# Half blocks put behind a condition, and wider matmuls in the experts' second product

## The chip, the cores and the metric

The kernel runs on one core of a Trainium2 chip. The metric is the device time of one execution in microseconds. Three runs of the kernel before took 5778.13, 5779.1 and 5784.61 us (median 5779.1). The engines are PE (TensorE, the matmuls), ACT (ScalarE), DVE (VectorE), POOL (GpSimd, which issues the gathers and scatters) and SP (SyncE, which issues the other transfers).

## The reference, cut to what matters

```python
attn = np.maximum((1/S) * z @ z.T, 0) ** 2       # 8 batches, S = 3072
x = (u * (attn @ v)).reshape(24576, 256)
h = x @ w_in; x = (h - np.tanh(h)) @ w_out       # 256 -> 2048 -> 256
e_idx = np.argmax(x @ w_gate, axis=1)            # one of 8 experts for each token
for e in range(8):
    mask = e_idx == e
    h = np.maximum(x[mask] @ w1[e], 0)           # 256 -> 1024
    out[mask] = gate_w[mask, None] * eom[mask, e, None] * (h @ w2[e])   # 1024 -> 256
```

The change touches only the last part, the experts.

## The kernel before, in words

**Stages.** Attention, the dense layer and the routing run chunk by chunk (48 chunks of 512 tokens) until about 4.45 ms. The routing writes each token's number into a table, sorted by expert. Then the experts run over blocks of that table: `NA` = 39 whole blocks of 512 tokens (i = 0 to 38), then `NHB` = 25 half blocks of 256 (i = 39 to 63). How many half blocks hold tokens depends on the data: 24576 - 39*512 = 4608 tokens are left, 18 half blocks if every expert's rest fills its blocks, and up to 7 more, since each of 8 experts may leave its last one part empty. `end[E-1]` is that count. The kernel before runs all 25; a half block without tokens reads and computes zeros, and its scatter drops the rows.

**Precision.** Each float32 operand is split into a high and a low part. A product is three matmuls: high by high, high by low, low by high.

**One block.** `b_load` fetches token numbers (SP), `x_load` gathers the tokens' rows (POOL, one DMA for each 128 tokens), `w_fetch` loads both weights (SP; a half block loads the second one whole and `w_split` splits it on ACT, DVE and POOL), `x_tr` transposes on PE and evacuates on ACT and DVE. Then come four groups g: `w1_mm` (12 matmuls; 512 columns wide in a whole block, 256 in a half one), `h_make` (the relu on ACT, the low part on DVE), `w2_mm` (for each of 2 features and each slice t of 128 tokens 3 matmuls of 256 columns: 24 in a whole block, 12 in a half one). `y_out` scales the result (ACT, one instruction for each slice) into `yo`, a tile with one buffer, and scatters it (POOL).

**What sets the order.** Every step is entered with a due time (`at(t, ...)`), and all steps are recorded in the order of these; the numbers are a plan, not measured. Every engine then runs its own instructions in that order. `w2_mm` of group g is due two groups behind `w1_mm` of g, so that between the last `w2_mm` of block i and the first of block i+1 stands one `w1_mm` group of block i+1.

**PSUM.** The result of `w2_mm` takes two banks in a whole block (two slices in each): `av0`, `av1` in the first five blocks, from then on these and `x20`, `x21` in turn; in a half block one bank, `x20` and `x21` in turn. `x_tr` and every second `w1_mm` share a buffer with the tag `sc`, so a `w1_mm` waits there until DVE has read the transposes (L795).

Of the kernel before, what the change touches and what calls it, by code (L numbers as in the profile page):

```python
# [5 lines left out]
F32 = mybir.dt.float32  # L6
F32R = mybir.dt.float32r
BF16 = mybir.dt.bfloat16
I32 = mybir.dt.int32
I64 = mybir.dt.int64  # L10
U16 = mybir.dt.uint16
AF = mybir.ActivationFunctionType
ALU = mybir.AluOpType
# [4 lines left out]
P = 128  # L18
FLOOR = 2.0**-15
CH = 512  # L20
# [5 lines left out]
    HA=(1, 7), L0=((), (0, 2, 4, 6, 8, 10)), LP=(0, 2, 4, 6, 8, 9, 10),  # L26
    G2=3.0, G3=5.0, GT=130.0, C0=6.0, C1=14.0, WL=14.0, CA=11.0, CP=15.0, ES=70.0,
    B0=30.0, B1=31.0, BL=14.0, XL=26.0, L1=2.0, L2=2.0, IO=10.0, SP=5.0, F0=24.0, F1=12.0,
    Z0=3.0, V0=40.0, V1=11.0, X1=1.0, RX=18.0,
)  # L30


# [28 lines left out]
def build(tc, u, v, z, w_in, w_out, w_gate, w_ogate, w1, w2, out):  # L61
    nc = tc.nc
    B, S, D = u.shape
    DQ = z.shape[2]
    N = B * S
    F = w_in.shape[1]
    E = w_gate.shape[1]
# [6 lines left out]
    NF2 = F2 // P  # L74
    CAP = N + CH
    HB = CH // 2
    NA = max(0, NCH - 2 - (E - 1))
    NHB = (N - NA * CH) // HB + E - 1
    assert ND == 2 and DQ == 64 and E == 8
    pb, pk, pc = _fit()  # L80

# [4 lines left out]
    tasks = []  # L86

    def at(t, fn, *a):
        tasks.append((t, len(tasks), fn, a))

    def flush():
        tasks.sort(key=lambda x: (x[0], x[1]))
        for _, _, fn, a in tasks:
            fn(*a)
        tasks.clear()
# [3 lines left out]
    def free_order(key, inst):  # L99

        i = inst.ins
        tc.declare_no_dep(i, group=key, reason="rows of different tokens")
        tc.add_to_no_dep_group(key, i)

    top = ExitStack()
    const = top.enter_context(tc.tile_pool(name="const", bufs=1))
# [40 lines left out]
    with ExitStack() as st:  # L147
# [3 lines left out]
        ps_s, ps_h, ps_a, ps_x = pp("ps_s", 1), pp("ps_h", 1), pp("ps_a", 1), pp("ps_x", 1)  # L151
# [411 lines left out]
        K = SCHED  # L563
# [11 lines left out]
        for b in range(B):  # L575
            for g in range(NG):
                if b == 0:
                    tz = -60.0 + g * K["Z0"]
                    tzt, tv = tz + 2, tz + K["V0"] + g * K["V1"]
                else:  # L580
                    t0 = (b * NG - 1) * TC
# [7 lines left out]
        for fp in range(NFP):  # L589
            t = K["C0"] + K["C1"] * fp  # L590
# [7 lines left out]
        for n, c in enumerate([c for c in range(3, NCH - 3) if c % NG != NG - 1][: 4 * E]):  # L598
            t = c * TC + K["ES"]
            at(t - 20.0, e_load, n // 4, n // 2 % 2, n % 2)  # L600
            at(t, e_split, n // 4, n // 2 % 2, n % 2)
        for c in range(NCH):
            t0 = c * TC
# [3 lines left out]
            for p in range(NJP):  # L607
                t = t0 + p * DJ
# [6 lines left out]
            for f in range(NFP):  # L615
                t = tm0 + f * DF
# [10 lines left out]
            n = int((te + 4.0 - EX - t0) // DJ) + 1  # L627
# [24 lines left out]
        less = [const.tile([1, E], F32, name=f"less{k}") for k in range(2)]  # L652
        it = const.tile([1, TBN], F32, name="it")
        iti = const.tile([1, TBN], I32, name="iti")
        tbe = [const.tile([1, TBN], I32, name=f"tbe{k}") for k in range(2)]
        tbb = [const.tile([1, TBN], I32, name=f"tbb{k}") for k in range(2)]

# [40 lines left out]
        def table_out(half):  # L698
            nb, end, sta, ex_, bs = (tb[n] for n in ("nb", "end", "sta", "ex", "bs"))
            tt, ts_ = nc.vector.tensor_tensor, nc.vector.tensor_scalar  # L700

            ts_(bs, bs, float(E * CAP), None, op0=ALU.min)
            nc.vector.tensor_copy(tbb[half], bs)
            ts_(ex_, ex_, float(E - 1), None, op0=ALU.min)
            nc.vector.tensor_copy(tbe[half], ex_)
            if not half:
                tt(sta, end, nb, op=ALU.subtract)
                ts_(sta, sta, float(NA), None, op0=ALU.min)
                ts_(end, end, float(NA), None, op0=ALU.min)
                tt(used[:, 0:E], end, sta, op=ALU.subtract)  # L710

        def block_table(t, half):

            at(t, table_counts, half)
            at(t + 2.0, table_steps, half)
            for e in range(E):
                at(t + 4.0 + e, table_expert, half, e)
            at(t + 13.0, table_out, half)
            return t + 13.0

        IDS, XG, WR, WB, XT, HS, YP = {}, {}, {}, {}, {}, {}, {}
        cp = {}

        def nt(i):
            return 4 if i < NA else 2
# [104 lines left out]

        def w2_mm(i, g):
            b2, hh = WB[i, 1], HS.pop((i, g))
            if g == 0:

                q = [int(k % 2 and k > 3) for k in range(NA)] + [NA % 2] * NHB
                pool, tags = ((ps_a, ("av0", "av1")), (ps_x, ("x20", "x21")))[q[i]]
                tags = tags if i < NA else tags[i % 2 : i % 2 + 1]
                YP[i] = [pool.tile([P, 2, D], F32, tag=x, name=f"y{x}") for x in tags]
            for j in range(2):
                f = 2 * g + j  # L840
                for t in range(nt(i)):
                    dst = YP[i][t // 2][:, t % 2]
                    for n, (a, w) in enumerate(((0, 0), (0, 1), (1, 0))):
                        nc.tensor.matmul(  # L844
                            dst, hh[:, a, j, t * P : (t + 1) * P], b2[:, w, f],
                            start=(f == 0 and n == 0 and t % 2 == 0),
                            stop=(f == NF2 - 1 and n == 2), skip_group_check=True,
                        )

        def y_out(i):  # L850
            ids, sc = IDS.pop(i)
            yo = cp[1].tile([P, 4, D], F32, tag="yo", name="yo")
            for t in range(nt(i)):
                nc.scalar.activation(  # L854
                    yo[:, t], YP[i][t // 2][:, t % 2], AF.Copy, scale=sc[:, t : t + 1]
                )
            for t in range(nt(i)):
                free_order("out", nc.gpsimd.indirect_dma_start(  # L858
                    out, bass.IndirectOffsetOnAxis(ap=ids[:, t : t + 1], axis=0),
                    yo[:, t], None, bounds_check=N - 1, oob_is_err=False,  # L860
                ))
            del YP[i], WB[i, 0], WB[i, 1], XT[i]
# [5 lines left out]
        t_table = T_ROUTED[NCH - 3] if NA else T_ROUTED[NCH - 1] - 13.0  # L868
        block_table(t_table + 0.1, 0)
        t_table = block_table(T_ROUTED[NCH - 1] + 0.2, 1)  # L870
        tC = NCH * TC + LA + 3.0
        t0 = tC + K["B0"]
        for i in range(NA + NHB):
            TB = 22.0 if i < NA else 11.0
            if i == NA:
                t0 = max(t0, t_table + 50.0)
            tf = t0 - (28 if i < NA else 20)
            at(max(t0 - K["F0"] if i < NA else t0 - K["F1"], tC), w_fetch, i, 0)
            at(max(t0 - 14.0 if i < NA else tf, tC), w_fetch, i, 1)
            at(max(tf - K["BL"], tC - 20.0), b_load, i)  # L880
            at(max(t0 - (K["XL"] if i < NA else 15.0), tC), x_load, i)
            first = i < min(NA, 3)
            for part in range(2 if i >= NA else 0):
                at(t0 - K["SP"] + 2.5 * part, w_split, i, part)
            if i == 0:
                at(t0 - 5.0 - K["X1"], x_tr, i)
            L2 = K["L1"] if i < NA else K["L2"]
            NG2 = NF2 // 2
            DB = TB / NG2
            for g in range(NG2):  # L890
                at(t0 + g * DB, w1_mm, i, g)
                at(t0 + g * DB + 0.4 * DB, h_make, i, g)
                at(t0 + (g + L2) * DB, w2_mm, i, g)
            at(t0 + (NG2 + L2 - 0.5) * DB, y_out, i)
            if i + 1 < NA + NHB:
                at(t0 + 2.7 * DB, x_tr, i + 1)
            t0 += K["B1"] if i < min(NA, 2) else TB

        late = [x for x in tasks if x[0] >= tC - 0.2]
        tasks[:] = [x for x in tasks if x[0] < tC - 0.2]  # L900
        with tc.manual_schedule():
# [4 lines left out]
        tasks.extend(late)  # L906
        with tc.manual_schedule():
            flush()
    top.close()


# [23 lines left out]
```

## Time and profile before

| what | value |
|---|---|
| three runs | 5778.13, 5779.1, 5784.61 us |
| the profiled execution | 5780.38 us, of it a span of 5778.7 us |
| PE busy | 5686.3 us (98%) |
| DVE, ACT, POOL busy | 4144.9, 3560.0, 1803.6 us (72%, 62%, 31%) |
| DMA | 872 MB, 151 GB/s in the mean |

PE is busy 98% of the span, and the other engines less in the experts' stage than ahead of it. A busy PE still holds matmuls of different cost, so the experts' stage is read by the starts of its matmul groups. In rows of the timeline the columns are the start in us, the duration in us, engine, line and operation, tiles and shape, count, and in brackets the idle time ahead of it with what ended it.

### The profile page before, as it was taken

To read this page: it belongs to the slowest core of one execution; us is meant where nothing else is said; L and a number is where in the kernel's file an instruction comes from. 1 tells how busy PE (TensorE), PEld (TensorE's weight loads), DVE (VectorE), ACT (ScalarE), POOL (GpSimd) and SP (SyncE) were. 2 spreads that over 40 slices of the span, in tenths; PEclk is the share of its full clock that TensorE was granted. 3 is DMA by queue.
4 is the path that set the end of the run, shared out by engine and by line. 5 is a ranking of instruction groups with operands and counts; after the bars stand their busy time and mean duration, and the time that the engine had idled before them with its cause. 6 is when DMAs were issued, how large, how long until landed. Compare 5 with 4: busy or idle time off the path is not lost. (4 is left out here: it accounts for less than half of the span.)

```text
span 5778.7 us, 73965 instructions
## 1 busy us (share of the span) xinstructions
PE 5686.3 (98%) x28444; PEld 4752.4 (82%) x28444; DVE 4144.9 (72%) x4921; ACT 3560.0 (62%) x3941; POOL 1803.6 (31%) x1174
## 2 busy tenths in 40 slices
PE   7999999999999999999999999999999999999999
PEld 5887888788888888888888788878887789999999
DVE  7888888888888888888888888888888532222233
ACT  5767776777677767777777767776766322222344
POOL 2224222322332224233322322242222233333355
PEclk9999999999999999999999999999999999999999
DMA  5333333333433333333333333343333566666687
GB/s 203 102 127 134 121 128 130 130 129 119 137 127 122 122 139 128 115 132 134 126 120 128 135 126 125 123 137 112 99 112 116 206 219 224 228 230 224 231 288 246
DMA packets 194065, 872.24 MB, mean 151 GB/s; under 512 B 37354, under 2 KB 78448, under 8 KB 130352
## 3 DMA queue, kind: packets, MB, share of 16 engines
q1 hardware_dynamic: 157936, 769.87, 38.2%
q0 software_dynamic: 35776, 97.63, 5.5%
q8 instruction: 225, 3.69, 0.3%
q14 instruction: 128, 1.05, 0.1%
HBM read 757.16 MB, written 99.49 MB: 148 GB/s over the span
## 5 line engine op out<-in xcount | busy, mean ns | idle before, releaser
L355 POOL TENSOR_TENSOR a<-r,a 128x1024 fp32r<-128x1024 f32 x328 | 789.5, 2407 | 2644.3 <-DVE a L352 2637.4
L400 PE MATMUL h<-x,ws 128*128 128x512 f32 x4608 | 1188.9, 397 | 18.5 <-DVE x L380 7.4
L341 ACT ACTIVATE r<-sc 128x1024 f32<-128x1024 f32 x576 | 586.6, 1018 | 976.8 <-PE sc L336 973.6
L400 PEld LDWEIGHTS h<-x,ws 128*128 128x128 f32 x4608 | 862.3, 188 | 225.3 <-DVE x L380 10.9
L371 PE MATMUL av<-a,v 128*128 128x512 f32 x2304 | 906.2, 393 | 11.4 <-DVE a L355 8.0
L370 PE MATMUL av<-a,v 128*128 128x512 f32 x2304 | 906.6, 394 | 2.2 <-ACT a L350 1.2
L372 PE MATMUL av<-a,v 128*128 128x512 f32 x2304 | 902.3, 392 | 0.0
L825 DVE SCALAR_TENSOR_TENSOR hh<-h,hh 128x1024 fp32r<-128x1024 f32 (+1 forms) x256 | 260.2, 1016 | 819.8 <-ACT hh L824 819.8
L824 ACT ACTIVATE hh<-h 128x1024 fp32r<-128x1024 f32 (+1 forms) x256 | 220.2, 860 | 820.1 <-PE h L813 820.1
L813 PE MATMUL h<-xt,b 128*128 128x512 f32 (+1 forms) x3072 | 622.1, 352 | 9.5 <-DVE xt L795 8.5
L342 ACT ACTIVATE r<-r 128x1024 f32<-128x1024 f32 x576 | 611.9, 1062 | 18.3
L439 PE MATMUL x<-g,ws 128*128 128x512 f32 x1536 | 611.7, 398 | 5.3 <-DVE g L426 3.0
L440 PE MATMUL x<-g,ws 128*128 128x512 f32 x1536 | 610.6, 398 | 6.1 <-DVE g L427 5.7
L408 DVE TENSOR_TENSOR gd<-h,gd 128x1024 f32<-128x1024 f32 x384 | 468.9, 1221 | 202.1 <-ACT gs L407 202.1
L441 PE MATMUL x<-g,ws 128*128 128x512 f32 x1536 | 607.8, 396 | 0.0
L813 PEld LDWEIGHTS h<-xt,b 128*128 128x128 f32 x3072 | 493.4, 190 | 81.9 <-DVE xt L795 13.6
L352 DVE CAST a<-r 128x1024 fp32r<-128x1024 f32 x470 | 335.6, 714 | 307.0 <-ACT r L342 186.0
L423 DVE SCALAR_TENSOR_TENSOR gq<-gt,gq 128x1024 f32<-128x1024 f32 x384 | 516.4, 1345 | 53.3 <-ACT gt L418 29.4
L424 DVE COPY_PREDICATED gq<-gm,gd 128x1024 f32<-128x1024 uint16 x384 | 518.4, 1350 | 13.2
L371 PEld LDWEIGHTS av<-a,v 128*128 128x128 f32 x2304 | 435.7, 189 | 108.2 <-DVE a L355 11.3
L370 PEld LDWEIGHTS av<-a,v 128*128 128x128 f32 x2304 | 435.1, 189 | 101.0 <-ACT a L350 3.6
L372 PEld LDWEIGHTS av<-a,v 128*128 128x128 f32 x2304 | 435.3, 189 | 93.9
(145 smaller groups left out, 9499.4 us busy)
## 6 DMA issues: line engine op xcount, KB each, us to landing
ws<-wsd SPq DMA_DIRECT2D x384, 1024.0 KB, 4.9
b<-wsp SPq DMA_DIRECT2D x103, 2048.0 KB, 8.2
wsp<-el POOLq DMA_DIRECT2D x32, 1024.0 KB, 8.5
x2d<-rows SPq DMA_DIRECT2D x48, 576.0 KB, 4.8
wr<-in_moe_w SPq DMA_DIRECT2D x25, 1024.0 KB, 9.6
vr<-in_v SPq DMA_DIRECT2D x48, 512.0 KB, 5.8
ur<-in_u SPq DMA_DIRECT2D x48, 512.0 KB, 5.8
er<-in_moe_w SPq DMA_DIRECT2D x32, 512.0 KB, 6.0
```

What stands on the lines that cost most here:

```text
L341: nc.scalar.activation(r, RR.pop((c, p)), AF.Relu, scale=1.0 / S)
L342: nc.scalar.activation(r, r, AF.Square)
L355: eng.tensor_tensor(a[:, 1], r, a[:, 0].bitcast(F32), op=ALU.subtract)
L370: nc.tensor.matmul(dst, vh, a[:, 0, k], start=(J == 0), stop=False)
L371: nc.tensor.matmul(dst, vh, a[:, 1, k], start=False, stop=False)
L372: nc.tensor.matmul(dst, vl, a[:, 0, k], start=False, stop=(J == 2 * NJP - 1))
L400: nc.tensor.matmul(ps, w, xx, start=(n == 0), stop=(n == 5))
L424: nc.vector.copy_predicated(q, m.bitcast(U16), d)
L439: nc.tensor.matmul(dst, wh, gg[:, 0, i], start=first, stop=False)
L440: nc.tensor.matmul(dst, wh, gg[:, 1, i], start=False, stop=False)
L441: nc.tensor.matmul(dst, wl, gg[:, 0, i], start=False, stop=last)
L813: nc.tensor.matmul(ps[:, j], w, xx, start=(n == 0 and (W == CH or j == 0)), stop=(n == 3 * ND - 1), skip_group_check=W < CH,)
```

## The change

The half blocks 57 to 63 (the last 7 of 25) are recorded behind the others and stand in a conditional part that runs when the count of half blocks is over `NHS` = 18. The count is copied to `nhb` when the table is made; all five engines read it into a register and branch by themselves. Everything of these blocks is in the conditional part, their loads and the first `x_tr` too. In `w2_mm` of the blocks from i = 5 on the high part of h meets high and low weights in one matmul of 512 columns, and the low part the high weights in one of 256; each slice has a bank of its own, so a whole block takes all four and a half block two, in turn. `y_out` adds the second half of the bank on DVE. In the last group of a block the matmuls go slice by slice. `y_out` is due earlier (`YO`), and the first half block 5.5 later.

```diff
@@ the due times
+    Z0=3.0, V0=40.0, V1=11.0, X1=1.0, RX=18.0, YO=1.0,
@@ w2_mm
+            wide = i >= min(NA, 5)
...
+            if wide and g == NF2 // 2 - 1:
+                order.sort(key=lambda x: x[1])
...
+                if wide:
+                    dst = YP[i][t]
+                    nc.tensor.matmul(
+                        dst, hi, b2[:, :, f], start=(f == 0), stop=(f == NF2 - 1),
+                        skip_group_check=True,
+                    )
+                    nc.tensor.matmul(
+                        dst[:, 0], lo, b2[:, 0, f], start=False, stop=(f == NF2 - 1),
+                        skip_group_check=True,
+                    )
+                    continue
@@ y_out
+                nc.scalar.activation(yo[:, t], y, AF.Copy, scale=sc[:, t : t + 1])
+                if wide:
+                    nc.vector.scalar_tensor_tensor(
+                        yo[:, t], YP[i][t][:, 1], sc[:, t : t + 1], yo[:, t],
+                        op0=ALU.mult, op1=ALU.add,
+                    )
@@ the plan of the blocks
+            if i == NA + NHS:
+                sure = list(tasks)
+                tasks.clear()
+                at(t0 - 0.3 * DB, x_tr, i)
             if i == NA:
-                t0 = max(t0, t_table + 50.0)
+                t0 = max(t0 + 5.5, t_table + 50.0)
...
-            at(t0 + (NG2 + L2 - 0.5) * DB, y_out, i)
-            if i + 1 < NA + NHB:
+            at(t0 + (NG2 - 1 + L2) * DB + K["YO"], y_out, i)
+            if i + 1 < NA + NHB and i + 1 != NA + NHS:
                 at(t0 + 2.7 * DB, x_tr, i + 1)
@@ the end
+        n = nc.values_load(nhb[0:1, 0:1], min_val=0, max_val=NHB)
+        with tc.If(n > NHS):
+            tasks.extend(rest)
+            with tc.manual_schedule():
+                flush()
```

Three places show what moves. In the rows `hh` is made by `h_make`, `yo` by `y_out`, `xt` by `x_tr`, `b1` by `w_split`; `out` is the scatter and `xg` the gather.

ACT at the turn from block 2 to block 3, before:

```order
L824 ACTIVATE hh_36686<-h2_36662 128x1024
L824 ACTIVATE hh_36726<-h2_36713 128x1024
L854 ACTIVATE yo_36740<-yav0_36476,scl_36223 128x256 x2
L854 ACTIVATE yo_36740<-yav1_36477,scl_36223 128x256 x2
L824 ACTIVATE hh_36796<-h2_36783 128x1024
```

And after:

```order
L828 ACTIVATE hh_36687<-h2_36663 128x1024
L878 ACTIVATE yo_36727<-yav0_36477,scl_36224 128x256 x2
L878 ACTIVATE yo_36727<-yav1_36478,scl_36224 128x256 x2
L828 ACTIVATE hh_36744<-h2_36714 128x1024
L828 ACTIVATE hh_36797<-h2_36784 128x1024
```

Block 2's `yo` has moved ahead of block 3's second `hh`; it is so at every turn of whole blocks.

ACT from the end of block 38 (whole) to `yo` of block 39 (half), before (`yo_45189` is block 38's, `yo_45325` block 39's):

```order
L824 ACTIVATE hh_45117<-h2_45104 128x2x256
L773 ACTIVATE b1_45170<-wr_44968 128x1024
L824 ACTIVATE hh_45173<-h2_45157 128x2x256
L794 ACTIVATE xt_45181<-xps_45182 128x2x256
L854 ACTIVATE yo_45189<-yav0_44920,scl_44722 128x256 x2
L854 ACTIVATE yo_45189<-yav1_44921,scl_44722 128x256 x2
L773 ACTIVATE b1_45170<-wr_44968 128x1024
L824 ACTIVATE hh_45233<-h2_45218 128x2x256
L824 ACTIVATE hh_45283<-h2_45270 128x2x256
L824 ACTIVATE hh_45322<-h2_45309 128x2x256
L854 ACTIVATE yo_45325<-yx21_45144,scl_44973 128x256 x2
```

And after (`yo_44228` and `yo_44425`):

```order
L878 ACTIVATE yo_44228<-yx21_44042,scl_43875 128x256
L828 ACTIVATE hh_44249<-h2_44215 128x2x256
L828 ACTIVATE hh_44276<-h2_44263 128x2x256
L777 ACTIVATE b1_44302<-wr_44148 128x1024
L828 ACTIVATE hh_44305<-h2_44289 128x2x256
L798 ACTIVATE xt_44313<-xps_44314 128x2x256
L777 ACTIVATE b1_44302<-wr_44148 128x1024
L828 ACTIVATE hh_44344<-h2_44329 128x2x256
L828 ACTIVATE hh_44390<-h2_44377 128x2x256
L878 ACTIVATE yo_44425<-yx20_44279,scl_44078 128x256
```

Between the two `yo` stand five `hh` and no longer three, with the transposes' `xt` and both `b1` between them too: the first `yo` has moved ahead of block 39's first `hh`.

POOL around the turn from block 56 to block 57, before (`out` of blocks 55, 56 and 57, `xg` of 58 and 59):

```order
L858 DMA out_0<-yo_48093,idb_47332 24576x256 x2
L742 DMA xg_48134<-x2d_61,idb_47851 128x288 x2
L775 TENSOR_TENSOR b1_48128<-wr_47890,b1_48128 128x1024
L858 DMA out_0<-yo_48266,idb_47505 24576x256 x2
L742 DMA xg_48307<-x2d_61,idb_48024 128x288 x2
L775 TENSOR_TENSOR b1_48301<-wr_48063,b1_48301 128x1024
L858 DMA out_0<-yo_48439,idb_47678 24576x256 x2
```

And after (`out` of 55 and 56, the branch, then `xg` of 57 and 58):

```order
L885 DMA out_0<-yo_46916,idb_46287 24576x256 x2
L885 DMA out_0<-yo_46996,idb_46447 24576x256 x2
L943 TENSOR_LOAD nhb_129
L944 COMPARE_AND_BRANCH
L746 DMA xg_47058<-x2d_61,idb_47034 128x288 x2
L746 DMA xg_47097<-x2d_61,idb_47045 128x288 x2
L779 TENSOR_TENSOR b1_47094<-wr_47056,b1_47094 128x1024
```

Before, block 57's gather is issued two blocks ahead of its use; after, it stands behind block 56's scatter and the branch.

## Rows read from the trace of the kernel before

**Rows 1.** Windows: stretch, length, busy by engine, granted clock, DMA share, GB/s.

```profile
4690.00:5440.00 750.00, 750.00 (x4859) 683.78 (x4858) 194.51 (x192) 206.68 (x286) 248.88 (x254) 1.00 0.65 229
5500.00:5745.00 245.00, 240.65 (x1975) 236.60 (x1974) 92.05 (x139) 109.05 (x179) 142.09 (x99) 1.00 0.89 297
```

**Rows 2.** DMA queue 0 from 5739.3, 5751.7 and 5764.1: packets, MB, share.

```profile
q0 software_dynamic: 192, 0.56, 28.9%
...
q0 software_dynamic: 96, 0.03, 1.0%
...
q0 software_dynamic: 192, 0.00, 0.9%
```

**Rows 3.** Timeline, a whole block: DVE's transposes, then PE's groups behind them.

```profile
5212.33 1.22 DVE L795 TENSOR_TENSOR xt<-xps,xt 128x1024 fp32r<-128x1024 f32 x1
...
5213.60 3.03 PE L813 MATMUL h<-xt,b 128*128 128x512 f32 x12
5216.47 3.04 PE L844 MATMUL yav<-b,hh 128*128 128x256 f32 x24
5219.34 2.91 PE L813 MATMUL h<-xt,b 128*128 128x512 f32 x12
5222.09 3.04 PE L844 MATMUL yav<-b,hh 128*128 128x256 f32 x24
```

**Rows 4.** Timeline of PE, a half block, from the transposes to the next w1 group.

```profile
5753.23 0.60 PE L790 MATMUL xps<-ident,xg 128*128 128x128 f32 x4
5753.58 1.67 PE L844 MATMUL yx<-b,hh 128*128 128x256 f32 x12
5755.47 1.69 PE L813 MATMUL h<-xt,b 128*128 128x256 f32 x12 [0.22 <-DVE xt L795]
```

**Rows 5.** Timeline at two turns among the first five blocks.

```profile
4613.03 3.15 PE L844 MATMUL yav<-b,hh 128*128 128x256 f32 x24 [1.91 <-ACT yo L854]
...
4638.00 1.56 ACT L854 ACTIVATE yo<-yav,scl 128x256 f32<-128x256 f32 x4
...
4638.89 4.62 PE L844 MATMUL yav<-b,hh 128*128 128x256 f32 x24 [1.84 <-ACT yo L854]
```

**Rows 6.** Timeline behind the first half block, and the window of its slow matmuls.

```profile
5475.26 0.84 ACT L854 ACTIVATE yo<-yx,scl 128x256 f32<-128x256 f32 x2 [2.81 <-DMA out<-yo,idb]
...
5479.63 2.93 PE L813 MATMUL h<-xt,b 128*128 128x256 f32 x12 [3.07 <-DVE xt L795]
5482.36 2.76 PE L844 MATMUL yx<-b,hh 128*128 128x256 f32 x12
5484.92 1.96 PE L813 MATMUL h<-xt,b 128*128 128x256 f32 x12
...
5479.60:5485.70 6.10, 6.07 (x28) 6.08 (x29) 0.69 (x1) 0.60 (x1) 4.20 (x3) 0.50 0.60 164
```

**Rows 7.** Timeline of the last block's end.

```profile
5768.52 3.03 PE L844 MATMUL yx<-b,hh 128*128 128x256 f32 x24
...
5771.64 0.84 ACT L854 ACTIVATE yo<-yx,scl 128x256 f32<-128x256 f32 x2 [2.32 <-PE yx L844]
...
5773.68 0.98 POOL L858 DMA_INDIRECT out<-yo,idb  x1 [0.30 <-issue]
```

**Rows 8.** A gather's issue, two of SP's issues, landing times of xg and idb.

```profile
5744.12 0.97 POOL L742 DMA_INDIRECT xg<-x2d,idb  x1 [0.30 <-issue]
...
5707.52 0.33 SPq L762 DMA_DIRECT2D b<-wsp  x1
5708.75 0.33 SPq L733 DMA_DIRECT2D idb<-table  x1
...
DMA to landing us min/median/max: 2.8/5.1/7.1
...
DMA to landing us min/median/max: 2.1/5.6/9.3
```

**Rows 9.** A group of DVE by shape in the half blocks' stage.

```profile
L825 DVE SCALAR_TENSOR_TENSOR hh<-h,hh 128x512 fp32r<-128x512 f32 x79 | 54.7, 692 | 133.4 <-ACT hh L824 133.4
```

More of the change, by code (lines that the diff above doesn't have):

```diff
@@ L28 @@
     B0=30.0, B1=31.0, BL=14.0, XL=26.0, L1=2.0, L2=2.0, IO=10.0, SP=5.0, F0=24.0, F1=12.0,
-    Z0=3.0, V0=40.0, V1=11.0, X1=1.0, RX=18.0,
+    Z0=3.0, V0=40.0, V1=11.0, X1=1.0, RX=18.0, YO=1.0,
 )
@@ L77, in build @@
     NA = max(0, NCH - 2 - (E - 1))
-    NHB = (N - NA * CH) // HB + E - 1
+    NHS = (N - NA * CH) // HB
+    NHB = NHS + E - 1
     assert ND == 2 and DQ == 64 and E == 8
@@ L654, in build @@
         iti = const.tile([1, TBN], I32, name="iti")
+        nhb = const.tile([1, 1], I32, name="nhb")
         tbe = [const.tile([1, TBN], I32, name=f"tbe{k}") for k in range(2)]
@@ L705, in table_out @@
             nc.vector.tensor_copy(tbe[half], ex_)
-            if not half:
+            if half:
+                nc.vector.tensor_copy(nhb, end[:, E - 1 : E])
+            else:
                 tt(sta, end, nb, op=ALU.subtract)
@@ L832, in w2_mm @@
             b2, hh = WB[i, 1], HS.pop((i, g))
[L833 to L839, printed above, removed]
-                f = 2 * g + j
[L841 to L848, printed above, removed]
+            wide = i >= min(NA, 5)
@@ new lines, in w2_mm @@
+            if g == 0 and not wide:
+                YP[i] = [ps_a.tile([P, 2, D], F32, tag=f"av{k}", name=f"yav{k}") for k in range(2)]
+            elif g == 0:
+                tags = [(ps_a, "av0"), (ps_a, "av1"), (ps_x, "x20"), (ps_x, "x21")]
+                tags = tags if i < NA else tags[i % 2 * 2 : i % 2 * 2 + 2]
+                YP[i] = [pool.tile([P, 2, D], F32, tag=x, name=f"y{x}") for pool, x in tags]
+            order = [(j, t) for j in range(2) for t in range(nt(i))]
+            if wide and g == NF2 // 2 - 1:
+                order.sort(key=lambda x: x[1])
@@ new lines, in w2_mm @@
+            for j, t in order:
+                f = 2 * g + j
+                hi, lo = (hh[:, a, j, t * P : (t + 1) * P] for a in range(2))
+                if wide:
[9 more added lines that the diff above has]
+                    continue
+                dst = YP[i][t // 2][:, t % 2]
+                for n, (h, w) in enumerate(((hi, 0), (hi, 1), (lo, 0))):
+                    nc.tensor.matmul(
+                        dst, h, b2[:, w, f],
+                        start=(f == 0 and n == 0 and t % 2 == 0),
+                        stop=(f == NF2 - 1 and n == 2), skip_group_check=True,
+                    )
@@ L853, in y_out @@
             for t in range(nt(i)):
-                nc.scalar.activation(
-                    yo[:, t], YP[i][t // 2][:, t % 2], AF.Copy, scale=sc[:, t : t + 1]
-                )
+                wide = len(YP[i]) == nt(i)
+                y = YP[i][t][:, 0] if wide else YP[i][t // 2][:, t % 2]
+                nc.scalar.activation(yo[:, t], y, AF.Copy, scale=sc[:, t : t + 1])
[3 more added lines that the diff above has]
+                        op0=ALU.mult, op1=ALU.add,
+                    )
             for t in range(nt(i)):
@@ L893, in build @@
                 at(t0 + (g + L2) * DB, w2_mm, i, g)
-            at(t0 + (NG2 + L2 - 0.5) * DB, y_out, i)
-            if i + 1 < NA + NHB:
+            at(t0 + (NG2 - 1 + L2) * DB + K["YO"], y_out, i)
+            if i + 1 < NA + NHB and i + 1 != NA + NHS:
                 at(t0 + 2.7 * DB, x_tr, i + 1)
             t0 += K["B1"] if i < min(NA, 2) else TB
+        rest = list(tasks)
+        tasks[:] = sure
         late = [x for x in tasks if x[0] >= tC - 0.2]
```

## The prediction

> **What bounds the kernel now.** I read the windows by stage first. In the whole blocks PE is busy for all of 750 us at a granted clock of 1.00, in the half blocks for 240.65 of 245 us [rows 1]: only PE's own work, and the few places where it stands still, can move the time. So I then read the starts of PE's groups in one block of each kind [rows 3, 4], the places with idle time in brackets [rows 5, 6], and the end of the last block [rows 7]. One question is not about time: are the seven half blocks needed on these inputs? Queue 0 carries nothing but POOL's gathers and scatters there. In a half block with both it moves 0.56 MB, which is 256 gathered rows of 1152 bytes and 256 scattered rows of 1024 (0.295 + 0.262). That is so still in the window from 5739.3, when block 60 is scattered. In block 61's window 0.03 MB are moved, about 25 rows, and in the window of the last two scatters 0.00 [rows 2]. So 23 half blocks hold tokens (39 to 61), the count is over 18, the branch is taken, and nothing is left out.
>
> **The change part by part.** The sum is made against the profiled execution (5780.4 us, 1.3 above the median).
>
> *The wide matmuls.* A w2 group of 24 matmuls of 256 columns lasts from 5216.47 to 5219.34, 2.87 us or 0.1196 each; a w1 group of 12 of 512 columns from 5219.34 to 5222.09, 2.75 us or 0.229 each [rows 3]. So two of 256 cost 0.239 and one of 512 costs 0.229: a feature and slice saves 0.010 us. A whole block has 32 of these (8 in each of 4 groups), a half block 16. Not all count. Behind the transposes the next w1 group waits for DVE's evacuation of them: it starts at 5213.60, and DVE ends at 12.33 + 1.22 = 5213.55 [rows 3]; in a half block PE already waits there [rows 4]. That chain does not get shorter, so in one of the four groups of each block PE waits out what the matmuls save. Left are 34 blocks x 24 + 25 x 12 = 1116 pairs: 11.2 us gained. The ends: another w1 group took 2.87 us for its 12 (from 5213.60 [rows 3]), 0.239 each, by which nothing is gained; all 1488 pairs would give 14.9. I take the value from the undisturbed group.
>
> The Trainium skill has a rule on this, in "TensorE: Matmul & The Clock Gate", section "Back-to-back issue gap": a warm matmul follows the last after its columns at 2.4 GHz plus about 2.5 ns. By it a pair would save 2.5 ns, and the term would be 2.8 us. The rows do not bear it out for these float32r matmuls: they show 0.1196 for 256 columns.
>
> *The output.* Each slice now has a DVE instruction behind its ACT one. DVE took 0.69 us for 512 columns [rows 9]; 0.35 to 0.69 for 256 as an estimate. DVE is busy 194.51 of 750 us in the whole blocks [rows 1], so the four fit in. What can be late is the bank: a whole block now takes all four, and the first w2 group of the next must wait for `yo`. Between them stands a w1 group of 2.75 us; the slices are finished one by one, and the last needs some 0.2 + 0.4 + 0.5 us behind its last matmul. I price that at nothing; the cover is 1.6 us.
>
> *The earlier `yo`.* At two turns among the first five blocks, which use one pair of banks, PE waits 1.91 and 1.84 us for ACT's `yo`, and the group behind the second takes 4.62 us where 3.15 was the other's time, 1.5 more [rows 5]. ACT had to make the next block's second `hh` first. In the new order `yo` stands ahead of that `hh`, so it can start when its matmuls end, 2.75 us before the banks are wanted, and lasts 1.56 [rows 5]. Gained: 1.91 + 1.84 + 1.5 = 5.2 us (3.7 if the slow group stays).
>
> *The turn to half blocks.* ACT waits 2.81 us with `yo` of block 39, because block 38's scatter still reads the one buffer; PE then stands for 3.07 us, and the next three groups take 2.93, 2.76 and 1.96 [rows 6] where 1.69, 1.67 and 1.69 are usual [rows 4]: 2.6 us more, at a granted clock of 0.50, the 1.2 GHz level [rows 6]. The shift by 5.5 puts block 38's `yo` ahead of block 39's first `hh`, so a whole block's four groups of both kinds lie between the two `yo`, over 12 us; four scatters (1.3 apart) and a landing fit in. Gained: 5.7 us (0 if the landing stays last).
>
> *The conditional part.* No engine waits for another at the branch; SP is through early and block 57's weights are there. But POOL runs in order, and behind block 56's scatter, the register and the branch stands block 57's gather. From the end of block 56's last matmul, by the last block's end: 5768.52 + 3.03 = 5771.55, and the second scatter's issue ends at 5773.68 + 0.98, so 3.1 us [rows 7] (the DVE step is new, but the first slice ends earlier). The read of the count and the branch: no row of POOL; SP's read of a table lies between two issues, 5707.52 + 0.33 and 5708.75, 0.9 [rows 8]; I take that, and 0.3, POOL's own distance between issues, as the low end. Two gathers: the second starts 0.3 + 1.27 later and lands after 5.1 (2.8 to 7.1) [rows 8]. From the transposes to the first w1 group 2.24 [rows 4]. Sum: 3.1 + 0.9 + 1.6 + 5.1 + 2.2 = 12.9. Block 56 is spared the transposes and their wait, 5755.47 - 5753.23 less a w2 group of 1.44 [rows 4]: 0.8. PE stands longer here than the 3.07 us behind which the clock was 0.50; the two prices seen for that are 1.5 and 2.6, I take 2.5. Lost: 14.6 us (10.7 with the low ends; 22.2 with the highest landing and 5.6 for code, below).
>
> *The end.* The blocks end with one more wait and branch: 0.5 us lost (0 to 2).
>
> Sum: -11.2 - 5.2 - 5.7 + 14.6 + 0.5 = -7.0; 5780.4 becomes 5773.4, and by the median 5779.1 - 7.0 = 5772.1, rounded to 5772.
>
> **The rivals.** *Short gap.* The gather lands fast in the emptied queue and all four groups count: -14.9 - 5.2 - 5.7 + 10.7 + 0.5 gives 5764.5. For it: in the gap fewer loads run than at 0.89 [rows 1]; against it: two weight loads are still under way, and rows 3 show DVE at the limit.
>
> *The pair is no cheaper.* If a 512-column matmul among 256-column ones costs the 0.239 of the slower group, 11.2 us are missing: 5783. The skill's rule above, with its 2.8 us, would come close to this (5780.5).
>
> *Code behind the branch.* If POOL must fetch its instructions anew, the price is about that of a small DMA, 5.6 us in the median [rows 8], and it lies wholly in the gap: 5777.7. The Trainium skill says so in "Runtime: NRT & Kernel Launch", section "Instruction fetch mechanics": a taken branch out of the loaded pages waits for a fetch. No run here shows it yet; the code stands directly behind the branch, which speaks against it.
>
> *The banks turn late (slower).* If at each of 33 turns of wide whole blocks ACT and DVE are late by more than the 1.6 us of cover, PE waits as in rows 5, some 1.9 us each: 63 us, 5835. Against it: the new order of ACT.
>
> *Nothing is run.* If the count were 18, seven blocks of 12.4 us and the gap would go: 5671. Rows 2 exclude it.
>
> **How the numbers follow.** Forecast 0.44 (own range 5766 to 5778), short gap 0.23, no cheaper pair 0.12, code 0.13, late banks 0.07, nothing run 0.01. The predicted time is 5772. 0.2% is 11.6 us, about what a measurement can tell from no change: faster is below 5767.5, slower above 5790.7. Faster: most of the short gap, a fifth of the forecast and the last, 0.30; slower: late banks and the tail of gap plus dear pairs, 0.11; the same 0.59. The range 5763 to 5784 leaves out late banks and the outer ends.
>
> **What would show it.** In the profile after: a w2 group of a whole block at 2.79 us; no wait for `yo` in the first blocks; no PE idle behind the first half block; one PE idle of about 12 us between blocks 56 and 57 ended by the gather, with a clock of 0.50 behind it; queue 0 in blocks 57 to 61 still at 0.56 MB. It is wrong if w2 groups stay at 2.87, if PE waits for DVE's `yo` at every turn, or if the gap is under 8 or over 20 us.

## The result, and the profile after

The changed kernel takes 5824.69 us (median of four runs, 5818.31 to 5828.75), the kernel before 5780.99 in the same session: a ratio of 1.0074, 95% interval [1.0057, 1.0092]. It is 44 us slower; the forecast was 5772, with a range up to 5784.

The waits of PE over the whole span, of the changed kernel (engine, line, what it waited for: us in total, times, longest):

```profile
PE h L817 <- DVE xt L799: 42.2, 44, 3.7
PE xps L794 <- DMA xg<-x2d,idb: 10.7, 2, 9.8
```

The second row is the gap at the branch, which was forecast. The first was not: at 44 places a `w1_mm` group waits for the transposes' evacuation (their copy out of PSUM by ACT and DVE). Most of it, 30.5 us at 30 places, is in the whole blocks between 4690 and 5440, where PE was busy for all of 750 us before [rows 1]. The same window now, with its columns as in rows 1:

```profile
4690.00:5440.00 750.00, 719.54 (x3677) 601.74 (x3676) 237.36 (x305) 211.57 (x274) 241.58 (x247) 1.00 0.62 217
```

PE stands still for 30 of the 750 us, at a granted clock of 1.00 in the mean. One whole block shows where. Timeline of PE, ACT, DVE and POOL around the transposes of block 28, after:

```profile
5206.94 0.39 PE L855 MATMUL yav<-b,hh 128*128 128x512 f32 x1
5207.17 0.28 PE L859 MATMUL yav<-b,hh 128*128 128x256 f32 x1
...
5209.76 2.95 PE L817 MATMUL h<-xt,b 128*128 128x512 f32 x12
5212.55 1.03 PE L794 MATMUL xps<-ident,xg 128*128 128x128 f32 x8
...
5216.93 0.96 PE L817 MATMUL h<-xt,b 128*128 128x512 f32 x3 [0.57 <-DVE xt L799]
```

```profile
5212.74 1.02 ACT L828 ACTIVATE hh<-h 128x1024 fp32r<-128x1024 f32 x1 [4.57 <-issue]
5213.80 1.23 DVE L829 SCALAR_TENSOR_TENSOR hh<-h,hh 128x1024 fp32r<-128x1024 f32 x1 [4.37 <-ACT hh L828]
5214.59 1.03 ACT L798 ACTIVATE xt<-xps 128x1024 fp32r<-128x1024 f32 x1 [0.82 <-PE xps L794]
```

```profile
5209.72 0.98 POOL L746 DMA_INDIRECT xg<-x2d,idb  x1 [0.30 <-issue]
5211.01 0.97 POOL L746 DMA_INDIRECT xg<-x2d,idb  x1 [0.30 <-issue]
5212.29 0.95 POOL L746 DMA_INDIRECT xg<-x2d,idb  x1 [0.30 <-issue]
5213.54 0.94 POOL L746 DMA_INDIRECT xg<-x2d,idb  x1 [0.30 <-issue]
```

The last transpose starts at 5213.31, and the `w2_mm` behind it follows without a break. ACT's copy of the transposes starts at 5214.59, 1.28 us behind it, having waited 0.82 us with nothing else to do: "PE xps" is what it waited for. In the kernel before ACT's copy comes 0.36 us behind the last transpose in every whole block from block 5 on. So TensorE's signal (the semaphore that tells ACT that the transposes are done) arrives about 0.9 us late here. ACT's own signal to DVE is on time in the same us: DVE's low part of `hh` starts at 5213.80, 0.03 behind the end of ACT's `hh`. One block of the kernel before (its last transpose starts at 5210.63):

```profile
5209.86 1.04 PE L790 MATMUL xps<-ident,xg 128*128 128x128 f32 x8
5210.03 0.99 POOL L858 DMA_INDIRECT out<-yo,idb  x1 [0.30 <-issue]
5210.98 1.02 ACT L794 ACTIVATE xt<-xps 128x1024 fp32r<-128x1024 f32 x1
5211.32 0.98 POOL L742 DMA_INDIRECT xg<-x2d,idb  x1 [0.30 <-issue]
```

In the changed kernel, from block 7 to block 37, the 0.36 has become 1.26 to 1.33, 1.95 to 2.02 or 2.65 to 2.72 (0.36 in block 8 alone), and the period of a whole block, 23.47 before, is 24.0 to 24.8 in most. POOL's rows tell what is new: four gathers (of a later block) lie around the transposes. Before, from block 7 on, the scatters lay there, and the gathers began behind ACT's copy.

Two other rows that the prediction asked for: the `w2_mm` group takes 5209.76 - 5206.94 = 2.82 (2.87 before [rows 3], 2.79 forecast); and no row of the waits names `yo`.

The account follows the starts of each block's transposes in the traces (column "after": changed kernel less kernel before, from block 2's transposes on, since the stage ahead of them differs by -2.3 to +3.8 us from one execution to the next). The other columns, e7 and e10, are the kernels of experiments 7 and 10, below. Each column is one traced execution.

| stretch | after | e7 | e10 |
|---|---|---|---|
| blocks 2 to 5 (the first turns) | -7.15 | -9.05 | -9.00 |
| whole blocks 5 to 38 | +38.35 | -2.80 | +0.08 |
| turn to half blocks (38 to 42) | -0.74 | -4.79 | -2.13 |
| half blocks 42 to 56 | -1.16 | -1.17 | +0.36 |
| branch (56 to 58) | +13.71 | -0.16 | +0.02 |
| 58 to the end | -0.72 | -0.78 | +0.14 |
| sum, us | +42.3 | -18.8 | -10.5 |

### The profile page after: what moved, and what is told of

It is laid out like the page before. It is cut to its first block, busy times and chain, and to the rows that moved or that the text cites. A ratio compares the mean times of both kernels' runs of the same rounds, so it can differ in the third digit from the quotient of the medians.

```text
span 5823.5 us, 71277 instructions
## 1 busy us (share of the span) xinstructions
PE 5685.6 (98%) x26956; PEld 4669.0 (80%) x26956; DVE 4225.3 (73%) x5108; ACT 3581.2 (61%) x3941; POOL 1806.5 (31%) x1174
## 5 line engine op out<-in xcount | busy, mean ns | idle before, releaser
L372 PEld LDWEIGHTS av<-a,v 128*128 128x128 f32 x2304 | 435.3, 189 | 110.4 <-DVE a L356 12.9
```

Of the source, the lines that this page charges most:

```text
L372: nc.tensor.matmul(dst, vh, a[:, 1, k], start=False, stop=False)
```

## The experiments

**1. The earlier output alone.**

```diff
-            at(t0 + (NG2 + L2 - 0.5) * DB, y_out, i)
+            at(t0 + (NG2 - 1 + L2) * DB + 1.0, y_out, i)
```

> The kernel before with one edit: the output step of each block is due earlier, as in the changed kernel. Theory A (gathers beside the transposes): the earlier output sends the scatters earlier, POOL then issues the gathers of a later block in the 4 us around the transposes, and ACT gets the transposes 0.9 to 2.3 us late; the period of a whole block rises from 23.47 to 24.0 to 24.8 us and the time to 5800 to 5820. Theory B (the wide matmuls behind the transposes are the cause): ACT's copy of the transposes stays 0.36 us behind the last of them, the period stays 23.47, and the time falls by the waits removed, to 5771 to 5778.

Measured: 5874.32 us, ratio 1.0155 [1.0138, 1.0172], twice the loss of the whole change, with narrow matmuls and no branch. Theory A holds in its direction, B falls; the time is 54 us over A's range. Waits of PE from 4690 to 5440, then POOL's first and last gather and ACT at one block, and the windows of the gap and of the time behind it:

```profile
PE h L813 <- DVE xt L795: 48.6, 27, 1.9
```

```profile
5195.97 0.98 POOL L742 DMA_INDIRECT xg<-x2d,idb  x1 [0.30 <-issue]
5199.78 0.94 POOL L742 DMA_INDIRECT xg<-x2d,idb  x1 [0.30 <-issue]
5200.81 1.02 ACT L824 ACTIVATE hh<-h 128x1024 fp32r<-128x1024 f32 x1 [6.32 <-PE xps L790]
5202.28 1.02 ACT L794 ACTIVATE xt<-xps 128x1024 fp32r<-128x1024 f32 x1 [0.44 <-remote]
```

```profile
5199.60:5204.60 5.00, 3.19 (x28) 2.99 (x25) 2.52 (x3) 2.05 (x2) 0.94 (x1) 1.00 0.31 91
5204.60:5211.00 6.40, 6.39 (x29) 5.43 (x30) 0.68 (x1) 1.02 (x1) 0.00 (x0) 0.73 0.21 38
```

The copy comes 2.6 us behind the last transpose (5199.66), and PE stands for 1.8 us a block. Here the `hh` ahead of it is late too: 1.9 us behind the start of the transposes, where it was 0.2 (5209.86 to 5210.06) in the kernel before. A block takes 25.4 to 27.1 us, over the 24.0 to 24.8 that were expected: PE stands longer, and the granted clock falls behind these gaps, to 0.73 in the window shown (part of it at the 1.2 GHz level, the rest at 2.4); in the changed kernel it was 1.00 in the mean from 4690 to 5440.

**2. No conditional part** (all 25 half blocks in one plan).

```diff
-            if i == NA + NHS:
-                sure = list(tasks)
-                tasks.clear()
...
-        with tc.If(n > NHS):
-            tasks.extend(rest)
```

> The changed kernel with all 25 half blocks in the one plan and no branch. It measures the conditional part: both theories expect 5824.7 less 13 to 16, so 5809 to 5812, with the whole blocks as late as before (24.0 to 24.8 us each). If the price were lost to something else, less than 8 us would come back.

Measured: 5807.6 us, ratio 1.0043 [1.0026, 1.0060]; 17 less than the changed kernel and 1.4 under the expected range. The trace shows 13.9 of it between blocks 56 and 58. The whole blocks are as late as before the edit.

**3. One gather buffer for whole blocks.**

```diff
-            xg = cp[2].tile([P, 4, ROW], F32, tag="xg", name="xg")
+            xg = (cp[1].tile([P, 4, ROW], F32, tag="xgw", name="xg") if i < NA
+                  else cp[2].tile([P, 2, ROW], F32, tag="xg", name="xg"))
```

> The changed kernel, but the gathered rows of whole blocks have one buffer and no longer two, so a gather can only start when the transposes before it have read that buffer. Theory A: with the gathers behind the transposes ACT gets them 0.36 us after the last, as in the kernel before; the period of a whole block falls to 23.3 to 23.5 and the time to 5780 to 5792. Theory B: the delay stays, 24.0 to 24.8 a block, 5820 to 5830. If the gather then lands too late for its block, PE waits for it: over 5830.

Measured: 5781.6 us, ratio 0.9999 [0.9989, 1.0008]: 43 us come back by moving the gathers alone. The same window, then ACT and POOL at one block (the last transpose starts at 5201.28):

```profile
4690.00:5440.00 750.00, 749.09 (x3842) 628.07 (x3842) 244.88 (x320) 217.56 (x288) 250.60 (x256) 1.00 0.65 227
```

```profile
5200.71 1.02 ACT L829 ACTIVATE hh<-h 128x1024 fp32r<-128x1024 f32 x1 [4.57 <-PE h L818]
5201.64 1.02 ACT L799 ACTIVATE xt<-xps 128x1024 fp32r<-128x1024 f32 x1
```

```profile
5196.41 0.99 POOL L886 DMA_INDIRECT out<-yo,idb  x1 [0.30 <-issue]
5203.86 0.98 POOL L747 DMA_INDIRECT xg<-x2d,idb  x1 [6.47 <-issue]
```

With one buffer a gather must wait until the transposes and DVE's `scl` have read it. The copy follows the last transpose by 0.36 us in every whole block from block 5 on, and the period is 23.38. One late signal is left, at the turn to half blocks: block 40's transposes (from 5452.92) meet a gather at 5452.81, ACT's copy comes 3.04 behind the last of them, and PE waits for the evacuation:

```profile
5457.66 2.93 PE L818 MATMUL h<-xt,b 128*128 128x256 f32 x12 [2.75 <-DVE xt L800]
```

**4. The output as late as before, in the changed kernel.**

```diff
-            at(t0 + (NG2 - 1 + L2) * DB + K["YO"], y_out, i)
+            at(t0 + (NG2 + L2 - 0.5) * DB, y_out, i)
```

> The changed kernel with the output step due as late as in the kernel before. Theory A: the scatters lie beside the transposes again and the gathers behind, ACT's copy is on time; but a whole block holds all four banks, and PE waits some 1.9 us for the output at each of 33 turns: 5840 to 5850. Theory B: both the late copy and the wait, 5870 to 5890.

Measured: 5948.11 us, ratio 1.0278 [1.0261, 1.0296], outside both expectations. PE's waits from 4690 to 5600:

```profile
PE yav L855 <- issue: 92.8, 33, 2.8
PE h L817 <- DVE xt L799: 1.7, 7, 0.4
```

The wait for the banks is 2.8 us at each of 33 turns, half as much again as the 1.9 taken, and the mean granted clock is 0.985. (The profile names no releaser for it; that it is the banks is read from the rows, where PE goes on just behind DVE's first slice of `yo`.) So the wide matmuls need the earlier output, and that brings the gathers along.

The evacuation is nearly on time, but not for A's reason: the scatters do not lie beside the transposes again. With PE held up, gathers lie around them from block 7 to block 37, the first issued 1.1 to 3.8 us ahead of the last transpose, and ACT's copy is on time in 16 of these 31 blocks and 0.3 to 0.7 late in the others. In block 13 (last transpose at 4877.48) the first gather stands 3.69 ahead of it, just as in experiment 1, and the copy 0.36 behind:

```profile
4873.79 0.98 POOL L746 DMA_INDIRECT xg<-x2d,idb  x1 [0.30 <-issue]
4876.72 1.03 PE L794 MATMUL xps<-ident,xg 128*128 128x128 f32 x8
4877.84 1.03 ACT L798 ACTIVATE xt<-xps 128x1024 fp32r<-128x1024 f32 x1
```

The `w1_mm` group ahead of these transposes is slower here (3.07 us from its start to theirs, 2.75 in experiment 1), so the two blocks are not alike in all else. But gathers around the transposes do not always make the signal late.

**5 and 6. What of the gathers does it?** Both start from experiment 1, whose delay is the largest and nearly constant.

```diff
-                nc.gpsimd.indirect_dma_start(xg[:, t, :], None, x2d[:, :], ...)
+                nc.gpsimd.dma_start(xg[:, t, :], x2d[t * P : (t + 1) * P, :])
```

> The first experiment's kernel (before, with the earlier output alone) with each gather replaced by a plain load of 128 rows of the same 1152 bytes, issued by POOL at the same place; the rows are not the routed ones, so the output is another. Theory C (any traffic into the gathered rows' tile at that moment makes TensorE's signal late): the signal stays 2.3 to 2.6 us late in whole blocks and the time 5860 to 5880. Theory D (it is the indirect gather on POOL): signals on time, ACT's copy 0.36 us behind the last transpose, 5770 to 5780.

```diff
-                        xg[:, t, d * (P + 32) : d * (P + 32) + P], ident,
+                        ident, ident,
```

> The first experiment's kernel with the transposes reading a constant tile and no longer the gathered rows, which leaves the tokens out of the products; the gathers, scatters and all else stay. Theory E (TensorE reads the gathered tile while DMA writes into its neighbour): the signal is on time and the time falls to 5770 to 5785. If what counts is only that gathers run at that moment, the delay stays: 5860 to 5880.

Measured: 5767.48 and 5763.74 us, one run each beside 5777.57 of the kernel before. In experiment 5 the bytes still land over the transposes (in blocks 7 to 37 from some 0.7 us ahead of the last one to 1.4 to 2.8 behind it; in experiment 1 to 2.6 to 3.3 behind), but POOL's four loads take 0.56 us each and are through about 1.7 ahead of it; the signal is on time. So the landing bytes alone don't do it. Whether it is the kind of transfer (theory D) or only that POOL is through earlier, this experiment does not tell. In experiment 6 POOL's rows stand where they stood, and the copy is on time:

```profile
5221.37 0.95 POOL L742 DMA_INDIRECT xg<-x2d,idb  x1 [0.30 <-issue]
5221.72 1.03 PE L790 MATMUL xps<-ident 128*128 128x128 f32 x8
5221.92 1.03 ACT L824 ACTIVATE hh<-h 128x1024 fp32r<-128x1024 f32 x1 [4.59 <-PE h L813]
5222.62 0.94 POOL L742 DMA_INDIRECT xg<-x2d,idb  x1 [0.31 <-issue]
5222.84 1.02 ACT L794 ACTIVATE xt<-xps 128x1024 fp32r<-128x1024 f32 x1
```

So in this kernel it takes both: a later block's gathers at that moment, and transposes that read the gathered tile. (These transposes do not wait for the gathers' semaphores either; reading and waiting went together.)

**7 and 8. Two kernels without the loss.** Experiment 7 joins the edits of 2 and 3. Experiment 8 keeps the conditional part, but with the last two half blocks only:

```diff
+    NSK = NHB - 2
...
-            if i == NA + NHS:
+            if i == NA + NSK:
...
-        with tc.If(n > NHS):
+        with tc.If(n > NSK):
```

> The changed kernel with one gather buffer for whole blocks and without the branch: the two edits of the second and third experiments together. If their gains add (43 and 17 us), 5764 to 5766, 0.3% under the kernel before; if the gap at the branch also hid something, 5766 to 5775.

> The changed kernel with one gather buffer for whole blocks, and with only the last two half blocks (62 and 63) in the conditional part, which runs when the count is over 23. The count is 23 by the queue rows of the kernel before, so nothing is behind the branch: two blocks of 12.33 us go and no gap comes. 5764 less 24.7, so 5738 to 5742. If the count were over 23, 5780.

Measured: 5764.4 us, ratio 0.9978 [0.9968, 0.9987], and 5740.42 us, ratio 0.9937 [0.9921, 0.9954]. Both as expected, and both beat both kernels. Experiment 8 is the fastest, 37 us under the kernel before: blocks 62 and 63 aren't run, and nothing waits at the branch. That also shows that the count is not over 23.

Block 40 of experiment 7 is another case against a rule by place alone. There (last transpose at 5453.53) the gathers stand as in experiment 3, 0.43 us ahead and 1.01 behind (there 0.44 and 0.98), and the signal is on time, where it was 2.7 us late in experiment 3:

```profile
5453.10 1.13 POOL L747 DMA_INDIRECT xg<-x2d,idb  x1 [0.30 <-issue]
5453.20 0.60 PE L795 MATMUL xps<-ident,xg 128*128 128x128 f32 x4
5453.90 0.59 ACT L799 ACTIVATE xt<-xps 128x512 fp32r<-128x512 f32 x1
```

**9, 12 and 13. Shifting the gathers.** Experiment 1 with one, two or six memsets ahead of each whole block's gathers:

```diff
+            if 0 < i < NA:
+                fill = cp[1].tile([P, 256], F32, tag="fill", name="fill")
+                nc.gpsimd.memset(fill, 0.0)
```

> The first experiment's kernel with a memset of 128x256 on POOL ahead of each whole block's gathers, an estimate of 0.3 to 0.8 us. In block 8 of the first experiment the gathers stood 0.43 us later than elsewhere and the signal was on time. Theory F (only the place of a gather's issue beside the last transpose counts): shifted by that much, the signal is on time in most blocks, 5775 to 5790. Theory G (a later block's gathers anywhere in these 4 us do it): late still, another amount, 5840 to 5890.

> The first experiment's kernel with two memsets ahead of each whole block's gathers, which by the ninth experiment (0.36 us for one, gathers 0.19 us later) moves the gathers 0.5 to 0.6 us. Theory F (the place of a gather's issue beside the last transpose counts): at that distance block 8 was on time in the first and ninth experiments, so most blocks are on time, 5775 to 5790. Theory G (gathers anywhere in these 4 us): late in most blocks, 5840 to 5890.

> The first experiment's kernel with six memsets ahead of each whole block's gathers, some 2 us later. Theory F: another gather now stands beside the last transpose, so late again in most blocks, 5840 to 5890. Theory G: the later the gathers, the fewer of their landings stand before the transposes, but two are still issued before the end of them; late, but by less than 2 us a block, 5800 to 5850.

Measured, one run each: 5880.65, 5771.15 and 5771.84 us. In experiment 1 the first gather is issued 3.69 us ahead of the last transpose; now 3.50, 2.76 and 1.29. At 3.50 all whole blocks from 7 to 37 but block 8 are late, at 2.76 and 1.29 none of them. (Experiment 9 moved the gathers by 0.19 us only, too little to test F.) Experiment 12, one block (last transpose at 5038.96):

```profile
5036.19 0.99 POOL L746 DMA_INDIRECT xg<-x2d,idb  x1 [0.53 <-issue]
5038.20 1.03 PE L794 MATMUL xps<-ident,xg 128*128 128x128 f32 x8
5038.39 1.03 ACT L828 ACTIVATE hh<-h 128x1024 fp32r<-128x1024 f32 x1 [4.59 <-issue]
5038.77 0.95 POOL L746 DMA_INDIRECT xg<-x2d,idb  x1 [0.31 <-issue]
5039.31 1.02 ACT L798 ACTIVATE xt<-xps 128x1024 fp32r<-128x1024 f32 x1
```

A gather is issued right across the end of the transposes, and the copy is on time. So G falls (gathers anywhere in these us), and so does F as it was put for experiment 13. What is left of F: in this kernel 0.9 us of shift decides over 100 us of time. The distance by itself is no rule: in block 6 the first gather stands 2.43 ahead in experiment 1 and 1.57 in experiment 12, and the signal is 4.7 and 1.0 us late.

**14 and 15. Less of each.** Experiment 1, with only the first quarter of the tokens' transposes reading the gathered rows, and with the fourth gather a plain load (of rows that aren't the routed ones):

```diff
-                        xg[:, t, d * (P + 32) : d * (P + 32) + P], ident,
+                        ident if t else xg[:, t, d * (P + 32) : d * (P + 32) + P], ident,
```

> The first experiment's kernel with two of a block's eight transposes reading the gathered rows (the first quarter of the tokens) and six reading a constant, which leaves three quarters of the tokens out of the products. Theory H (the wait on the gathers' semaphores by TensorE's weight loads is enough): late as in the first experiment, 5860 to 5880. Theory E (reading the gathered tile while others land slows it): two reads of eight make it late by a quarter at most, 5775 to 5800.

```diff
+                if t == 3:
+                    nc.gpsimd.dma_start(xg[:, t, :], x2d[t * P : (t + 1) * P, :])
+                    continue
```

> The first experiment's kernel with the fourth gather of each block, the one issued 0.12 us behind the last transpose, replaced by a plain load of as many rows. Theory F: the signal is on time in most blocks, 5775 to 5790. Theory G: late still, by the three that are left, 5830 to 5880.

Measured, one run each: 5874.34 and 5829.41 us. Reading a quarter is as bad as reading all: the time is as H expects, and E falls. Without the fourth gather the copy is still 2.0 to 2.1 us behind; PE stands for 45.4 us instead of 48.6 between 4690 and 5440. What it gives back is mostly the clock: 1.00 in that window, 0.95 in experiment 1. So the gather beside the last transpose is not the cause by itself.

**10 and 11. Two terms by themselves.** Experiment 10 is the kernel before with the edits of 1 and 3 alone; experiment 11 is experiment 7 with this:

```diff
-                t0 = max(t0 + 5.5, t_table + 50.0)
+                t0 = max(t0, t_table + 50.0)
```

> The kernel before with two edits: the earlier output and one gather buffer for whole blocks; no wide matmuls, no shift, no branch. If the waits at the first turns are what the earlier output gives (9 us in the third experiment's rows) it takes 5777.6 less 9, so 5767 to 5771; the seventh experiment's 5764.4 then leaves 4 to 5 us to the wide matmuls, as the group rows say (0.09 us a whole block, 0.085 a half block), and not 11.

> The seventh experiment's kernel with the half blocks' due times not moved by 5.5. If the shift only moved the wait at the turn to the next block, as the rows of the third experiment show, the time stays within 2 us of 5764.4; by the prediction's term it would be 5.7 us longer, 5770.

Measured: 5768.78 us, ratio 0.9976 [0.9967, 0.9986], and 5770.37 us, ratio 0.9979 [0.9970, 0.9989]. By time the two can't be told from experiment 7 (0.9978). By the traces they can: from block 38 to 42 experiment 7 gains 4.79 us on the kernel before and experiment 11 loses 1.66, so the shift is worth 6.45 us beside wide matmuls, and what was expected of experiment 11 by the third experiment's rows was wrong. What PE waits for there without it:

```profile
PE yx L856 <- DVE yo L881: 3.7, 1, 3.7
```

## Why the prediction was wrong, step by step

**What bounds the kernel, and the count of 23.** Both right: PE alone sets the time there, and so 1 to 2 us of waiting in each block come through in full.

**The step that failed: the earlier `yo`.** It priced the waits that go (5.2 us) and nothing that the move sets off. The gain was even larger, 9.05 us in e7: the two turns that it named gave 5.7, and a third place was left out (3.3), block 2's transposes, where PE had waited 1.5 us for gathers that POOL issued behind block 0's four scatters, with slow matmuls after it. But an earlier `yo` sends four scatters earlier, POOL runs in order, and the gathers behind them had until then been held back to just behind the transposes. The prediction followed POOL only around the branch. The text ahead of it says that the other engines are busy less in the experts' stage than ahead of it; POOL is not: 58.05 of 250 us from 4200 to 4450, but 248.88 of 750 and 142.09 of 245 later [rows 1]. Experiment 1 shows this step alone costing 92 us, experiment 3 that 43 us come back when the gathers are put back. Why gathers around the transposes make TensorE's signal late stays open. None of the rivals was this; the slower one (late banks) named another mechanism, which experiment 4 shows to be real, at 2.8 us a turn, but not in this kernel.

**The wide matmuls: right direction, mis-sized.** Forecast 11.2 us; e7 against e10 gives 2.9 in whole blocks 5 to 38 and 1.5 in half blocks 42 to 56, at that rate 2.7 in all 25 half blocks: 5 to 6 us, half of the forecast. By time experiments 7 and 10 can't be told apart, so this rests on the traces. A `w2_mm` group between two `w1_mm` groups is 2.810 us where it was 2.872 (over 90 groups each from 4690 to 5410, experiment 3 and before), so a pair saves 0.0078 and not 0.010, 0.19 in a whole block. But its four `w1_mm` groups give 0.10 of that back: those between two `w2_mm` groups went from 2.785 to 2.809 in the mean, the one ahead of the transposes from 2.754 to 2.789. What is left is 0.09 a block. The price of 0.229 for 512 columns was a group's own mean and did not carry over. That the group behind the transposes gains nothing was right: 2.95 in both. By the formula of the Trainium skill that the prediction used ("TensorE: Matmul & The Clock Gate", "Back-to-back issue gap"), which the page gives for an isolated matmul, the term was 2.8 us; the rows lie between the two.

**The shift at the turn to half blocks.** Forecast 5.7 against the kernel before; against it the turn gains 4.79 in experiment 7, and 2.13 in experiment 10, which has no shift. The 6.45 between experiments 7 and 11 are more because without the shift the wide matmuls bring the wait for DVE's `yo` shown above, which the forecast did not have. In the changed kernel only 0.7 is seen: a late signal at block 40's transposes takes the rest, as the row of experiment 3 shows.

**The conditional part: right.** Forecast 14.6, measured 13.7. Timeline of POOL and PE at the branch, after:

```profile
5716.98 0.98 POOL L885 DMA_INDIRECT out<-yo,idb  x1 [5.83 <-DVE yo L880]
5718.27 2.02 POOL L885 DMA_INDIRECT out<-yo,idb  x1 [0.30 <-issue]
5720.60 0.98 POOL L746 DMA_INDIRECT xg<-x2d,idb  x1 [0.30 <-issue]
5721.89 0.97 POOL L746 DMA_INDIRECT xg<-x2d,idb  x1 [0.31 <-issue]
...
5726.16 1.09 PE L794 MATMUL xps<-ident,xg 128*128 128x128 f32 x4 [9.78 <-DMA xg<-x2d,idb]
```

The order of events is as forecast. The gather stands 0.3 us behind the scatter, the low end: the branch adds nothing that can be seen, and the read of the count (0.51 us, at 5717.5) lies beside the scatters. The second scatter takes 2.02 where 0.98 was taken. That is not the branch: DVE's share of the weight split (5718.21, 1.23 us) lies over it, and in the kernel before each of 22 scatters that lay 0.96 us under such an instruction took 1.84. From the second gather's issue to the transposes it is 4.3 us where 5.1 was taken. From the end of block 56's last matmul to the first `w1_mm` it is 11.6 us where 12.9 was taken; the next 24 matmuls take 5.8 us where 2.9 is usual, 2.9 more where 2.5 was taken, at a granted clock of 0.50 from 5726.1 to 5732. So the rival of code fetched behind the branch falls. The Trainium skill's rule on it ("Runtime: NRT & Kernel Launch", "Instruction fetch mechanics") is for a taken branch to code that is not yet loaded; here the code stands directly behind the branch, and no run here shows such a fetch.

**The end.** Forecast +0.5, measured 0.1: from block 58 to the end the changed kernel gains 0.72 us and experiment 7, which has no branch there, 0.78.

**The sum.** With the measured terms and without the late signals, the forecast would have been nearly no change: -9.05 - 2.8 - 4.8 - 1.2 + 13.7 - 0.7 = -4.9 us. The late signals make it +42: 41.2 in whole blocks 5 to 38, 1.9 at the turn into block 5, 4.1 at the turn to half blocks.

## What to carry to other kernels

When a step is moved earlier, follow every queue that it was holding back, to the end: what starts earlier behind it, and what does that then run beside? A gather that is only held back by what happens to stand ahead of it in POOL's queue has no fixed place; tie it to an event (here one buffer fewer) where its place matters. A conditional part that is taken costs a drained pipeline, 14 us here, so cut it where the count leaves it untaken, as experiment 8 does for these inputs.

## What the runs showed of the hardware that was not expected

TensorE's signal to ACT can come late, 0.9 to 2.4 us in whole blocks 7 to 37 of the changed kernel and of experiment 1, while the matmuls behind it start on time by their rows. In experiment 1's kernel it takes transposes that read a gathered tile (experiment 6; a quarter of them is enough, experiment 14) and a later block's gathers at a certain place around them (experiments 3, 12 and 13). Whether the gathers must be indirect is not shown: experiment 5's plain loads were also through earlier. The two together are not always enough. In that kernel a shift of 0.9 us decides (experiments 1 and 12), but with the gathers at the same place the signal was on time in block 13 of experiment 4 and in block 40 of experiment 7, and late in block 40 of experiment 3. What holds it is open: neither the landing bytes (experiment 5), nor a gather issued across the end of the transposes (experiment 12), nor the fourth gather alone (experiment 15) explains it, and in experiment 1 the signal of the `w1_mm` group ahead, which reads no gathered rows, was late as well.

A rival that no experiment tested is that TensorE itself is held there, and not only its signal: the ends of matmuls are modelled in these profiles. Block 6 of experiment 1, where the signal is latest (4.7 us; the last transpose starts at 4666.98), speaks for it. PE's rows stop there inside the `w2_mm` group behind the transposes, and no releaser is named; so they do in block 6 of experiments 9, 14 and 15.

```profile
4670.27 0.40 PE L844 MATMUL yx<-b,hh 128*128 128x256 f32 x2 [1.10 <-issue]
```

A DMA's issue on POOL takes longer while DVE splits weights: a scatter took 0.97 to 1.03 us without such an instruction over it, 1.84 with 0.96 us of overlap (the kernel before) and 2.02 with 1.17 (at the branch).
